# k and q projected together in three column chunks after the first FFN stage, with two G banks summed beside them

## The chip, the cores and the metric

The kernel runs on one core of a Trainium2 chip. A core has a matrix engine (TensorE, "PE" in the profile, with its weight loads as "PEld"), a vector engine (VectorE, "DVE"), a scalar engine for activation functions (ScalarE, "ACT"), a general engine (GpSimd, "POOL") and a queue engine (SyncE, "SP") that issues most transfers. TensorE writes its sums into eight PSUM banks of 128 partitions by 512 fp32 values. Sixteen DMA engines move data between DRAM and the on-chip SBUF. The metric is the device time of one execution in microseconds; lower is better.

## What is computed

For 2048 tokens x of width 640 (bf16) the output is a gated mix of a linear attention block with 32 heads of width 20 and a GEGLU feed-forward block with a hidden width of 1728:

```
qkv = x @ wqkv                                  # 640 -> 3*640
phi(t) = where(t > 0, t + 1, exp(t)) + 1e-6
kv  = sum over tokens of phi(k)^T v   (per head, 20x20);   z = sum over tokens of phi(k)
o   = (phi(q) @ kv) / (phi(q) . z + 1e-6)       (per head)
a   = o @ wo
b   = (gelu(x @ w_gate) * (x @ w_up)) @ w_down
g   = sigmoid(sum(x * gate_w));   out = g * a + (1 - g) * b
```

## The kernel before

**How it is tiled.** Tokens come in 16 tiles `t` of 128 and four quarters `q` of 512; the width 640 is five K-slices `dk` of 128; the hidden width is 14 f-tiles `ft`, the last of 64 columns. Two forms of x are needed: with tokens on partitions (`x_all`, `x_sb`) and transposed (`xT`). Quarters 1 to 3 of `xT` come from transposing DMA loads; quarter 0 is transposed on TensorE (`transpose_x`, L139) and copied out of PSUM by VectorE (K-slices 0 and 1) and ScalarE (2 to 4).

**v is never projected.** Since kv = phi(k)^T (x wv), the kernel sums G = x^T phi(k) over all tokens (`g_units`, L250), 640 by 640 in five row blocks and two column chunks of 512 and 128, one PSUM bank each, with 16 matmuls per bank. Then it multiplies by wv in head groups under a mask (`phase_KV`), and by wo (`phase_M`), which gives the matrix `M` that phi(q) is multiplied with in the end. z is summed on VectorE by 15 additions of [128 x 640] (`phase_Z`, L268) and replicated over partitions by a matmul with ones (`phase_Zrep`, L274). The denominators (`phase_D`) scale phi(q), which is then transposed by DMA into `pqT`.

**The feed-forward.** `phase_E(q, ft)` (L163) projects gate and up columns of an f-tile for one quarter: five matmuls of 512 columns into each of two banks, gelu on ScalarE, product on VectorE. `phase_FT` (quarters 0 to 2) and `phase_F` (quarter 3) sum the attention part and w_down into one bank and scale by 1 - g. The denominator's scale holds g/(1-g).

**k and q.** `phase_K(st)` (L206) projects one token tile's k in column chunks of 512 and 129; the 129th column of the second chunk is gate_w, so that x . gate_w comes out beside k, and exp of its negative goes to `eneg`. `phase_Q(st)` (L242) does q in 512 and 128. Each chunk passes through `phi` (L178): exp on ScalarE (L180), min and add on VectorE (L182), max and add from PSUM on VectorE (L185).

**The order of the work.** A planner orders each engine's instructions when the program is built, starting from the order in which they are written; inside `tc.manual_schedule` TensorE keeps the written order. It runs:

1. six warm-up matmuls on constants (`NWARM`, L117), which need no data;
2. `k_first` (L212), in written order: transposes of token tiles 0 and 1 with one filler matmul between them, k's first column chunk of both tiles K-slice by K-slice while wk arrives in three pieces (L95), the gate row turned into a column by a transpose (L231) and five POOL copies (L235), the second chunks, transposes of tiles 2 and 3;
3. k of tiles 2 and 3, q of tiles 0 to 3, then E of quarter 0 (14 f-tiles);
4. k of tiles 4 to 15, then q of tiles 4 to 15 with G's matmuls between them (a twelfth of G's columns after each tile) and the z additions, z's replication inside the last part of G;
5. KV, E of quarter 1 with M and the denominators, FT of quarter 0, and then E and FT or F by turns.

The transfers are issued in this order on SyncE's queue: x tile 0; wk in three pieces; x tiles 2 and 3; wq; gate and up weights in column pieces of 512, 512 and 640; their last 64 columns (`wgu`); three transposing loads; x of quarters 1 to 3; wv, wo, w_down. ScalarE's queue issues x tile 1 and the gate row.

## Time and profile before

| what | value |
|---|---|
| time, median of 3 runs | 279.5 us (279.43 to 279.55) |
| the profiled execution | 279.5 us, span 277.7 us from first to last instruction |
| TensorE busy | 272.2 us (98%) |
| VectorE busy | 143.3 us (52%) |
| ScalarE busy | 76.1 us (27%) |
| first transpose starts, first k matmul starts | 3.89 us, 5.14 us |
| E of quarter 0 | 17.84 to 46.97 us |
| KV starts | 101.63 us |
| transfers | 23.58 MB, mean 85 GB/s over the span |

How to read it: times of rows are microseconds from the start of the span. TensorE's matmuls are pipelined, so the length of one (379 ns for 512 columns) is longer than the interval between two; the interval is what a stage costs. VectorE's instructions also overlap by some tens of nanoseconds. The chain of waits follows the work that ended last back to the start; where its rows adjoin and name TensorE alone, TensorE sets the time.

### The profile page before, as it was taken

To read this page: it belongs to the slowest core of one execution; us is meant where nothing else is said; L and a number is where in the kernel's file an instruction comes from. 1 tells how busy PE (TensorE), PEld (TensorE's weight loads), DVE (VectorE), ACT (ScalarE), POOL (GpSimd) and SP (SyncE) were. 2 spreads that over 40 slices of the span, in tenths; PEclk is the share of its full clock that TensorE was granted. 3 is DMA by queue.
4 is the path that set the end of the run, shared out by engine and by line. 5 is a ranking of instruction groups with operands and counts; after the bars stand their busy time and mean duration, and the time that the engine had idled before them with its cause. 6 is when DMAs were issued, how large, how long until landed. Compare 5 with 4: busy or idle time off the path is not lost.

```text
span 277.7 us, 3993 instructions
## 1 busy us (share of the span) xinstructions
PE 272.2 (98%) x1522; PEld 139.0 (50%) x1548; DVE 143.3 (52%) x317; ACT 76.1 (27%) x167; POOL 5.2 (2%) x18
## 2 busy tenths in 40 slices
PE   8999999999999999999999999999999999999995
PEld 3554444555454584544444444444444444445774
DVE  0793223899944369999999542221112332101011
ACT  3662323764333352442100123210012222000100
POOL 5000000000000000000000000000000000000000
PEclk9999999999999999999999999999999999999999
DMA  7999999200100005343223540001112000021301
GB/s 217 360 355 205 235 341 287 96 2 0 1 4 0 0 2 142 69 113 75 51 50 69 104 133 3 0 0 29 30 38 94 2 0 0 19 40 38 118 26 47
DMA packets 43818, 23.58 MB, mean 85 GB/s; under 512 B 30808, under 2 KB 43672, under 8 KB 43800
## 3 DMA queue, kind: packets, MB, share of 16 engines
q1 hardware_dynamic: 43646, 23.17, 31.9%
q8 instruction: 12, 0.20, 0.3%
q10 hardware_dynamic: 154, 0.17, 0.2%
q14 instruction: 6, 0.05, 0.1%
HBM read 13.32 MB, written 2.63 MB: 57 GB/s over the span
## 4 chain that ended last, share of the span: by engine, by line
PE 96%; DMA 1%; ACT 1%; issue 1%; DVE 0%
PE ps_u L155 20%; PE ps_g L155 20%; PE ps_acc L378 16%; PE ps_q L192 8%; PE ps_G L255 8%; PE ps_k L192 7%; PE ps_acc L375 6%; PE ps_acc L398 5%; PE ps_acc L395 2%; PE ps_gu L155 2%; DMA x_all<-in_A_x_dram 1%; PE ps_k L218 1%; PE ps_m L332 1%; PE ps_kv L304 1%; ACT phi_e L180 0%
## 5 line engine op out<-in xcount | busy, mean ns | idle before, releaser
L160 ACT ACTIVATE gl<-ps_g 128x512 bf16<-128x512 f32 x52 | 31.1, 597 | 112.1 <-PE ps_g L155 111.3
L155 PEld LDWEIGHTS <-wu 128*128 128x128 bf16 x260 | 25.5, 98 | 30.7
L155 PEld LDWEIGHTS <-wg 128*128 128x128 bf16 x260 | 25.2, 98 | 29.1 <-issue 0.3
L161 DVE TENSOR_TENSOR hT_158<-ps_u,gl 128x512 bf16<-128x512 f32 x26 | 17.9, 690 | 31.9 <-PE ps_u L155 31.9
L378 PEld LDWEIGHTS <-wd 128*128 128x128 bf16 x210 | 20.5, 98 | 24.8
L378 PE MATMUL ps_acc<-hT_158,wd 128*128 128x512 bf16 x137 | 31.7, 379 | 0.2
L381 DVE TENSOR_TENSOR oT<-ps_acc,omg_rep 128x512 bf16<-128x512 f32 x15 | 10.3, 687 | 36.7 <-PE ps_acc L378 32.8
L161 DVE TENSOR_TENSOR hT_1371<-ps_u,gl 128x512 bf16<-128x512 f32 x26 | 17.8, 685 | 19.1 <-PE ps_u L155 19.1
L182 DVE TENSOR_SCALAR phi_m<-phi_e 128x512 bf16<-128x512 bf16 x64 | 12.9, 237 | 15.4 <-ACT phi_e L180 15.2
L180 ACT ACTIVATE phi_e<-ps_q 128x512 bf16<-128x512 f32 (+1 forms) x32 | 12.4, 435 | 21.6 <-PE ps_q L192 21.1
L398 PE MATMUL ps_acc<-wd,hT_1371 128*128 128x320 bf16 (+1 forms) x126 | 16.7, 284 | 0.0
L155 PE MATMUL ps_g<-xT_89,wg 128*128 128x512 bf16 x62 | 16.0, 379 | 0.2
L155 PE MATMUL ps_u<-xT_88,wu 128*128 128x512 bf16 x65 | 16.2, 379 | 0.0
L155 PE MATMUL ps_u<-xT_90,wu 128*128 128x512 bf16 x65 | 16.2, 379 | 0.0
L155 PE MATMUL ps_u<-xT_89,wu 128*128 128x512 bf16 x65 | 16.1, 379 | 0.0
L155 PE MATMUL ps_u<-xT_91,wu 128*128 128x512 bf16 x65 | 16.1, 379 | 0.0
L155 PE MATMUL ps_g<-xT_88,wg 128*128 128x512 bf16 x63 | 16.0, 379 | 0.1
L155 PE MATMUL ps_g<-xT_90,wg 128*128 128x512 bf16 x62 | 16.0, 379 | 0.2
L155 PE MATMUL ps_g<-xT_91,wg 128*128 128x512 bf16 x62 | 16.0, 379 | 0.2
L378 PE MATMUL ps_acc<-hT_1371,wd 128*128 128x512 bf16 x68 | 15.8, 379 | 0.1
L255 PEld LDWEIGHTS <-x_all 128*128 128x128 bf16 x160 | 12.0, 98 | 7.2
L180 ACT ACTIVATE phi_e<-ps_k 128x512 bf16<-128x512 f32 (+1 forms) x32 | 12.8, 439 | 7.5 <-PE ps_k L192 4.3
(142 smaller groups left out, 301.0 us busy)
## 6 DMA issues: line engine op xcount, KB each, us to landing
wd<-in_B_w_down_dram SPq DMA_DIRECT2D x1, 2080.0 KB
x_all<-in_A_x_dram SPq DMA_DIRECT2D x3, 640.0 KB, 4.8
out_dram<-o_q SPq DMA_DIRECT2D x3, 640.0 KB
wg<-in_B_w_gate_dram SPq DMA_DIRECT2D x2, 640.0 KB
wu<-in_B_w_up_dram SPq DMA_DIRECT2D x2, 640.0 KB, 10.2
wq<-in_A_wqkv_dram SPq DMA_DIRECT2D x1, 800.0 KB
wg<-in_B_w_gate_dram SPq DMA_DIRECT2D x1, 800.0 KB
wu<-in_B_w_up_dram SPq DMA_DIRECT2D x1, 800.0 KB
```

The source lines that it names most:

```text
L155: nc.tensor.matmul(ps[:, t0 : t0 + tw], lhsT=w[:, dk, ft * P : (ft + 1) * P], rhs=xT[q][:, dk, t0 : t0 + tw], start=(dk == 0), stop=(dk == ...
L160: nc.scalar.activation(out=gl[:], in_=psg[:], func=ACT.Gelu_apprx_tanh)
L161: nc.vector.tensor_tensor(out=hT_cur[q][:, ft, :], in0=psu[:], in1=gl[:], op=ALU.mult)
L180: nc.scalar.activation(out=e[:, :width], in_=src, func=ACT.Exp)
L182: nc.vector.tensor_scalar(out=m[:, :width], in0=e[:, :width], scalar1=1.0, scalar2=EPS, op0=ALU.min, op1=ALU.add,)
L192: nc.tensor.matmul(ps[:, 0 : hi - lo], lhsT=xT[q][:, dk, sl * P : (sl + 1) * P], rhs=w[:, dk, lo:hi], start=(dk == 0), stop=(dk == ND - 1),)
L255: nc.tensor.matmul(gp[:, 0 : hi - lo], lhsT=x_all[:, st, ct * P : (ct + 1) * P], rhs=pk[st][:, lo:hi], start=(st == 0), stop=(st == NT - 1),)
L375: nc.tensor.matmul(acc[:], lhsT=M["sb"][:, dk, ds], rhs=pqT[q][:, dk, :], start=(dk == 0), stop=False)
L378: nc.tensor.matmul(acc[:], lhsT=wd[:, ft, ds], rhs=hT[:, ft, :], start=False, stop=(ft == NF - 1))
L381: nc.vector.tensor_tensor(out=oT[:, 0:QW], in0=acc[:], in1=gsc["rep"][:, q * QW : (q + 1) * QW], op=ALU.mult)
L395: nc.tensor.matmul(acc[:, 0 : hi - lo], lhsT=pqT[q][:, dk, ts], rhs=M["sb"][:, dk, lo:hi], start=(dk == 0), stop=False)
L398: nc.tensor.matmul(acc[:, 0 : hi - lo], lhsT=hT[:, ft, ts], rhs=wd[:, ft, lo:hi], start=False, stop=(ft == NF - 1))
```

## The change

Quarter 0's E comes first and all of k and q after it, in one loop. wk, the gate column and wq become one tile `wqk` of 1281 columns, and `phase_KQ(st)` projects a token tile's k, gate and q in three column chunks of 512, 512 and 257, five matmuls each; phi's exp and min-add run per chunk, and the max-add is split where k ends and q begins. Beside this loop, two of G's ten banks are summed, one tile behind; the other eight follow when all k are done, and z is replicated after G. The transposes of quarter 0 go by pairs of token tiles into two banks with three copies (two on VectorE, one on ScalarE), and there is no written order for TensorE any more. The first two f-tiles of E run in halves of 256 tokens. There are seven warm-up matmuls.

On SyncE's queue stand now: x of tiles 0 and 1 in one transfer; 256 columns each of the gate and up weights; x of tiles 2 and 3; the further columns; `wgu`; wk; the gate column, element by element; the three transposing loads; wq; the rest as before. ScalarE's queue issues none. The ScalarE table that is loaded at the start is gelu's. `M`'s two tiles lie in one.

In the built program, the planner places one z addition beside each token tile of the new loop, from the second tile on, and z's replication between the last G matmul and KV. VectorE's second copy of a transposed pair waits for ScalarE's copy from the same bank.

```diff
-    NWARM = 6
+    NWARM = 7
...
-    wk = ov.tile([P, ND, D + P], BF16, name="wk", tag="slab_c")
-    wq = ov.tile([P, ND, D], BF16, name="wq", tag="slab_d")
+    WQK = 2 * D + 1
+    wqk = ov.tile([P, ND, WQK], BF16, name="wqk", tag="slab_c")
...
-    nc.scalar.dma_start(out=x_sb[0][:, 1, :], in_=x_view[:, 1, :])
-    nc.scalar.dma_start(out=gw5[:], in_=gate_w.rearrange("(k p) -> k p", p=P))
-    dma(out=x_sb[0][:, 0, :], in_=x_view[:, 0, :])
-    for lo, hi in ((0, 1), (1, 3), (3, 5)):
-        dma(out=wk[:, lo:hi, 0:D], in_=wqkv_v[:, lo:hi, D : 2 * D])
+    dma(out=x_sb[0][:, 0:2, :], in_=x_view[:, 0:2, :])
+    dma(out=wg[:, :, 0:256], in_=wg_v[:, :, 0:256])
+    dma(out=wu[:, :, 0:256], in_=wu_v[:, :, 0:256])
     dma(out=x_sb[0][:, 2:4, :], in_=x_view[:, 2:4, :])
-    dma(out=wq[:], in_=wqkv_v[:, :, 0:D])
...
-    for lo, hi in ((0, 512), (512, 1024), (1024, FM)):
+    for lo, hi in ((256, 512), (512, 1024), (1024, FM)):
...
+    dma(out=wqk[:, :, 0:D], in_=wqkv_v[:, :, D : 2 * D])
+    with nc.allow_non_contiguous_dma(reason="tiny gate_w column load"):
+        dma(out=wqk[:, :, D : D + 1], in_=gate_w.rearrange("(k p o) -> p k o", p=P, o=1))
     for q in (1, 2, 3):
         nc.sync.dma_start_transpose(out=xT[q][:, :, :], in_=x2[q * QW : (q + 1) * QW, :])
+    dma(out=wqk[:, :, D + 1 : WQK], in_=wqkv_v[:, :, 0:D])
...
+    def transpose_x(pair):
+        t0 = 2 * pair
+        tpa = psum.tile([P, 2 * QW], BF16, name="tp_a", tag="ps")
+        tpb = psum.tile([P, 2 * QW], BF16, name="tp_b", tag="ps")
+        c0 = t0 * P
+        for dk in range(ND):
+            tp, o = (tpa, dk * 2 * P) if dk < 2 else (tpb, (dk - 2) * 2 * P)
+            for i in range(2):
+                nc.tensor.transpose(
+                    tp[:, o + i * P : o + (i + 1) * P], x_sb[0][:, t0 + i, dk * P : (dk + 1) * P], ident[:]
+                )
...
+    def phase_KQ(st):
+        dst = (pk[st], pq[st])
+        for ci, (lo, hi) in enumerate(((0, QW), (QW, 2 * QW), (2 * QW, WQK))):
+            w = hi - lo
+            ps = ps_tile("ps_kq")
+            proj(ps, st, lo, hi)
+            e = work.tile([P, QW], BF16, name="phi_e")
+            nc.scalar.activation(out=e[:, 0:w], in_=ps[:, 0:w], func=ACT.Exp)
+            m = work.tile([P, QW], BF16, name="phi_m")
+            nc.vector.tensor_scalar(
+                out=m[:, 0:w], in0=e[:, 0:w], scalar1=1.0, scalar2=EPS, op0=ALU.min, op1=ALU.add,
             )
+            if ci == 1:
+                nc.scalar.activation(
+                    out=eneg[:, st : st + 1], in_=ps[:, D - QW : D - QW + 1], func=ACT.Exp, scale=-1.0
+                )
+            for i, base in ((0, 0), (1, D + 1)):
+                a, z = max(lo, base), min(hi, base + D)
+                if a < z:
+                    nc.vector.scalar_tensor_tensor(
+                        out=dst[i][:, a - base : z - base], in0=ps[:, a - lo : z - lo], scalar=0.0,
+                        in1=m[:, a - lo : z - lo], op0=ALU.max, op1=ALU.add,
+                    )
...
-    with tc.manual_schedule(engines={mybir.EngineType.PE}):
-        k_first()
-    for st in (2, 3):
-        phase_K(st)
-    for st in range(4):
-        phase_Q(st)
-    for ft in range(NF):
+    transpose_x(0)
+    e01 = [(ps_tile("ps_g"), ps_tile("ps_u")) for _ in range(2)]
+    for ft in range(2):
+        e_mm(e01[ft][0], wg, ft, 0, 0, 256)
+    e_mm(e01[0][1], wu, 0, 0, 0, 256)
+    transpose_x(1)
+    e_mm(e01[1][1], wu, 1, 0, 0, 256)
+    for ft in range(2):
+        e_mm(e01[ft][0], wg, ft, 0, 256, 256)
+        e_mm(e01[ft][1], wu, ft, 0, 256, 256)
+        e_out(0, ft, *e01[ft])
+    for ft in range(2, NF):
         phase_E(0, ft)
-    for st in range(4, NT):
-        phase_K(st)
+
+    early = [(ps_tile("ps_G"), ct) for ct in range(2)]
+    for st in range(NT):
+        phase_KQ(st)
+        if st > 0:
+            for gp, ct in early:
+                g_mm(gp, ct, st - 1, 0, QW)
+    for gp, ct in early:
+        g_mm(gp, ct, NT - 1, 0, QW)
+        g_out(gp, ct, 0, QW)
     phase_gate()
-    gu = g_units()
...
+    for st in range(NT):
+        phase_Z(st)
+    for i, (ct, lo, hi) in enumerate([(ct, 0, QW) for ct in range(2, ND)] + [(ct, QW, D) for ct in range(ND)]):
+        gp = ps_tile("ps_G")
+        for st in range(NT):
+            g_mm(gp, ct, st, lo, hi)
+        g_out(gp, ct, lo, hi)
     phase_Zrep()
-    for w in gu:
-        pass
     phase_KV(0, 4)
```

## The prediction

> **What bounds the kernel now.** I read the busy times first, then the chain of waits in order of time, then single matmuls of the first ten microseconds, then VectorE's timeline and the transfers. Busy times and the chain both say TensorE:
>
> ```profile
> PE 272.2 (98%) x1522; PEld 139.0 (50%) x1548; DVE 143.3 (52%) x317; ACT 76.1 (27%) x167; POOL 5.2 (2%) x18
> ```
>
> ```profile
> 0.81 3.03 DMA x_all<-in_A_x_dram
> 3.89 0.71 PE tp_x L145 x5
> ...
> 16.75 1.09 PE ps_q L192 x8
> 17.84 1.08 PE ps_g L155 x5
> ...
> 46.97 1.58 PE ps_k L192 x11
> ...
> 62.23 1.09 PE ps_k L192 x8
> 63.32 1.36 PE ps_q L192 x10
> ...
> 97.95 1.73 PE ps_G L255 x31
> ...
> 101.63 1.10 PE ps_kv L304 x20
> ...
> 270.28 1.90 PE ps_acc L398 x14
> ```
>
> The columns are start, length and work. Five 512-column matmuls take 1.08 us, so 215.8 ns each; 14 of 320 columns take 1.90, 135.7 each; 31 of 128 columns take 1.73, 55.8 each. Counting with these prices, the first E stage (135 x 215.8 = 29.13 us) runs from 17.84 to 46.97 and the stage of q and G from 63.32 to 101.63 without a hole. So no time is to be won by removing waits after 17.84: only the columns that TensorE streams, and the start, can move the end.
>
> The start I put into one number, TensorE's "zero": the moment from which an unbroken full-speed stream would have produced the same position. At 17.84 the k and q of four token tiles are done. One tile of k costs (63.32 - 46.97)/12 = 1.363 us, one of q 1.36; four of both cost 10.89. The zero of the kernel before is 17.84 - 10.89 = 6.95 us. It holds everything lost at the start: loads, transposes, and the slow clock, which shows in the starts of single matmuls:
>
> ```profile
> 6.42 0.93 PE L218 MATMUL ps_k<-wk,xT_88 128*128 128x512 bf16 x3
> ...
> 6.75 0.60 PE L218 MATMUL ps_k<-wk,xT_88 128*128 128x512 bf16 x2
> ...
> 6.97 0.38 PE L218 MATMUL ps_k<-wk,xT_88 128*128 128x512 bf16 x1
> ```
>
> These are tails of one group, cut at different moments: starts at 6.42, 6.75, 6.97, so the interval falls from about 0.43 (5.14 to 5.57) to 0.22 us. Full speed comes near 6.7, 5.9 us after the first warm-up matmul at 0.85.
>
> **Columns streamed (k and q together).** Removed per tile: 1.363 + 1.36 = 2.72 us in 20 matmuls. Added: ten of 512 (2.158) and five of 257 columns; 257 lies between 128 (55.8) and 320 (135.7), so 109.6 ns each, 0.548. The sum 2.706 saves 0.017 a tile, 16 tiles: **-0.25 us**. G keeps its 80 + 80 matmuls. Twenty matmuls of the first two f-tiles become forty of 256 columns (109.2 by the same line): **+0.05 us**.
>
> **The start.** Out go the K-slice order, the two transfers on ScalarE's queue (x tile 1, gate row), the gate's transpose, five POOL copies that a k matmul awaited, and a filler matmul between transposes; all that is inside 6.95. SyncE's queue now carries x of tiles 0-1 (320 KB), two 256-column pieces of wg and wu (320 KB each), x of tiles 2-3, then the rest. Transposes begin when x lands; x tile 0 landed at 3.84, and the seventh warm-up matmul ends at 0.85 + 7 x 0.427 = 3.84, so I take 3.87. Ten transposes at 0.107 (five took 0.50 before the next start) end at 4.94. VectorE copies 512 columns (288 ns for 256 and 160 for 5, so about 0.42) until 4.95, and the first gate-projection matmul starts at 5.05 once wg is in: k's first weights landed 2.9 us after issue at 1.27, with 0.49 MB up to them; 0.16 MB more makes about 4.9. Ten matmuls of 256, 0.213 each until 6.7, then 0.109, end at 7.0; five of wu end at 7.55. The next thing late is x of tiles 2-3:
>
> ```profile
> x_all<-in_A_x_dram SPq DMA_DIRECT2D x1, 320.0 KB, 5.2
> ...
> wk<-in_A_wqkv_dram SPq DMA_DIRECT2D x1, 160.0 KB, 2.9
> ...
> omg_d<-omg_all SPq DMA_DIRECT2D x1, 8.0 KB, 10.7
> ```
>
> Before, it was issued at 2.74 and landed 5.2 later, 7.94, as the end of 1.47 MB. Now it ends 1.31 MB: 0.16 MB less at 380 GB/s is 7.5. But wg and wu come in 512-byte pieces, which no row shows. 320 KB cost 0.9 us by bytes at 365 GB/s; if each piece cost what a 1024-byte piece does (SyncE pushed 640 of those per 1.79 us), 1.79. The two wgu transfers, 640 pieces of 128 bytes each, fit into the last microsecond before the transposing loads (windows of 21 to 22 us), at most 0.5 each; a line from there to 1.79 gives 1.05 at 512 bytes. That is 0.15 too much, twice: landing at 7.8, bounds 7.5 and 9.3. From there: ten transposes at 0.056 (0.56), ScalarE's copy (starts 0.25 later, 0.39), and only then VectorE's second copy of that bank, which waits for ScalarE (0.42); behind it stand the later projection matmuls. That is 1.65 us to 9.45, with 24 matmuls of 256 done (2.62): zero at 6.83, bounds 6.5 and 8.3. Against 6.95: **-0.12 us**, bounds -0.45 and +1.35. Nothing of E starves later: f-tile 4 is due near 15.5, its columns land by 14.
>
> The Trainium skill ("TensorE: Matmul & The Clock Gate", Part 1 and Part 4) speaks against this: full clock follows a busy window of about 3.4 us, and transposes don't count as busy, so the pause of 1.2 us in true matmuls could push the switch a window later, to about 10 us. By that rule the zero would be about 8.1 and the sum +0.95 us instead of -0.3. The trace of before shows a pause with a filler inside it, and no case without.
>
> **The load of wqk.** wk moves behind E's weights, the gate column becomes 640 two-byte pieces, wq stands behind three transposing loads. The windows' bytes reach the 6.72 MB ahead of those loads at 22.0 us, and they end at 32.0. Now 0.82 MB less is ahead (-2.2) and four 512-byte transfers (+0.6): 20.4. The gate lies between 0.5 (a 128-byte transfer of 640 pieces) and 3.3 (640/2048 of the 10.7 that omg_d's 2048 pieces took to land); I take 1.0, nearer the first, since that transfer also reads DRAM into SBUF. Then 10.0, wq 2.2, and 1.4 until it is seen: 35.0. The second column chunk of tile 0 needs it at 6.83 + 29.18 + 1.08 = 37.1. Cost **0**, slack 2.1; at 3.3 it is late by 0.2. Everything on PE's queue stands behind that wait. The other loads (x 4-15, wv, wo, wd) slip by about a microsecond; wv's first use is at 101. "DMA: Bandwidth & Descriptors" (Rules for kernel authors) says that a non-contiguous last dimension becomes one descriptor per element; it has no price for that.
>
> **VectorE in the joint stage.** Six banks are left, and per tile eight instructions follow each other:
>
> ```profile
> 50.78 0.39 DVE L182 TENSOR_SCALAR phi_m<-phi_e 128x512 bf16<-128x512 bf16 x2
> 51.08 0.82 DVE L271 TENSOR_TENSOR zacc<-zacc,pk_77 128x640 f32<-128x640 f32 x1
> 51.81 0.88 DVE L185 SCALAR_TENSOR_TENSOR pk_77<-ps_k,phi_m 128x512 bf16<-128x512 f32 x2
> 52.61 0.59 DVE L182 TENSOR_SCALAR phi_m<-phi_e 128x512 bf16<-128x512 bf16 x3
> ```
>
> Start to start, not by length: 512 + 128 of phi_m 0.30 (0.20 + 0.10), z's add 0.73, 512 + 128 of the max-add 0.80 (0.60 + 0.20). By the same slopes 257 of phi_m is 0.13, 383 and 257 of the max-add 0.47 and 0.33. Sum 0.20 + 0.20 + 0.13 + 0.60 + 0.20 + 0.47 + 0.33 + 0.73 = 2.87 us a tile (the planner puts z's add beside each tile). TensorE needs 2.706 + 2 x 0.216 = 3.14. VectorE just fits; a bank is back about 2.3 us after its last matmul and wanted again after 6.3 - 1.1. Cost **0**; with the lengths instead of the intervals (3.54), +0.40 x 16 = 6.4. ScalarE: 2 x 0.60 + 0.17 + 0.39 = 1.76 a tile; its table load (1.28) at the seam is covered by five free banks.
>
> **After G.** z's replication now stands right before KV, so VectorE's denominators start about 1.9 us later than before against TensorE. It is busy from 100.6 to 154.5, and its first copy of a final sum (152.3) comes 14 us after that sum is done. 1.9 later, the second E group of 155 still finds a bank. **0**.
>
> **Sum.** -0.25 + 0.05 - 0.12 = -0.32 us. The profiled execution took 279.5 with a span of 277.7, 1.8 around it, and equals the median of 279.5: 279.5 - 0.3 = **279.2 us**. That is inside 0.2% (0.56 us), about what a measurement can tell from no change.
>
> **Rivals.**
> 1. Slower: the clock. The point is whether transposes alone from 3.87 to 5.05 keep the clock's count going. For it: full speed needed 5.9 us, and the filler matmul is gone. Against it: TensorE stands idle less than before (before: 0.48 us ahead of the first transpose). If the count starts again at 5.05, the first 30 half-width matmuls and ten transposes run at half speed up to 10.9: zero 8.1 to 8.4, +1.0 to +1.3, **280.6**. 27%.
> 2. Slower: the gate's pieces. Every microsecond beyond 3.1 is one of stall at 37.1. Should they take as long as omg_d's whole 10.7, 286.8; half of that, 281.4. 12%.
> 3. Slower: VectorE at full lengths, 285.6. 6%; the intervals speak against it.
> 4. Faster: wg and wu at byte speed, zero 6.5: -0.45 - 0.2 = -0.65, **278.85**. For it: wgu's pieces were quick. 18%.
> 5. No change, the sum above: 37%.
>
> The range takes in 1, 4, 5 and the nearer half of 2: 278.8 to 281.4; the likeliest alone is 278.95 to 280.05. Faster 0.18, same 0.37, slower 0.45.
>
> **What would show it.** Right: the first projection matmul near 5.05, matmuls of 256 columns at 0.11 from 6.7, the second transposes at 7.8, E's end near 36.0, the joint stage 3.14 us a tile with no wait on VectorE, G's end straight into KV. Wrong: 0.21 intervals past 7.5 (rival 1), a hole before the second chunk of tile 0 with wqk as its releaser (2), TensorE waiting on phi's max-add (3), the second transposes past 8.5.

## The result and the profile after

The changed kernel takes 280.45 us (median of 6 runs, 280.17 to 280.76), the kernel before 279.52 in the same series (6 runs, 279.10 to 280.11). The ratio is 1.0031 with a 95% interval of 1.0018 to 1.0044: 0.9 us slower, where 0.3 us faster was forecast. The profiled execution took 280.49 us with a span of 278.8. A second series, of 12 runs, gave 1.0026 (1.0007 to 1.0044). Times and ratios in this document leave out one slow execution, of 486.2 us at a mean granted clock of 0.559, in the first run with x ahead of the up weights.

TensorE's busy time is nearly what it was (272.4 us against 272.2), so 0.9 of the 1.1 us by which the span grew is time in which it stands idle. Page of the changed kernel, busy time, share and instructions by engine:

```profile
PE 272.4 (98%) x1463; PEld 139.4 (50%) x1487; DVE 143.9 (52%) x300; ACT 72.2 (26%) x148; POOL 4.5 (2%) x13
```

The chain of waits of the changed kernel (start, length, work) answers the rows shown of before:

```profile
2.40 6.06 DMA x_all<-in_A_x_dram
8.50 0.40 PE tp_a L146 x4
...
35.80 1.09 PE ps_gu L166 x5
...
86.20 0.70 DVE pk_79 L216
86.95 3.61 PE ps_G L224 x16
...
102.64 1.10 PE ps_kv L272 x20
...
271.29 1.90 PE ps_acc L366 x14
```

Three readings. First, the chain no longer begins with x's first tile and TensorE, but with the load of token tiles 2 and 3, which lands at 8.46 us. Second, E ends at 35.80 + 1.09 = 36.89, so the zero is 36.89 - 29.18 = 7.71 us, where 6.95 stood before and 6.83 was forecast. (A row of the chain begins where the work before it ends, 0.17 us behind the start that the timeline gives for E; the zeros in this document are all read from chains, as the 6.95 was.) Third, between E and G stands VectorE, and it releases a matmul of G at 86.95. KV starts at 102.64, 1.01 later than before (101.63), and the same 1.01 is still there near the end (271.29 against 270.28): nothing is lost or won after KV.

TensorE's timeline at the start of the changed kernel (start, length, matmuls; in brackets the idle time ahead and what ended it):

```profile
5.14 1.65 PE L166 MATMUL ps_g<-xT_87,wg 128*128 128x256 bf16 x10
7.57 0.72 PE L166 MATMUL ps_u<-xT_87,wu 128*128 128x256 bf16 x5 [0.78 <-DMA wu<-in_B_w_up_dram]
8.50 0.40 PE L146 MATMUL tp_a<-ident,x_all 128*128 128x128 bf16 x4 [0.21 <-DMA x_all<-in_A_x_dram]
```

E starts at 5.14 (5.05 forecast) and its first ten matmuls are done by 6.8 (7.0 forecast). Then TensorE waits for the up weights' piece and again for x.

At the other end of the stage, TensorE's timeline around token tile 15:

```profile
86.17 0.59 PE L224 MATMUL ps_G<-pk_79,x_all 128*128 128x512 bf16 x2
86.95 0.59 PE L224 MATMUL ps_G<-pk_79,x_all 128*128 128x512 bf16 x2 [0.18 <-DVE pk_79 L216]
```

The second pair starts 0.78 after the first, in place of two times 0.216: a wait of 0.35 us for VectorE's max-add of tile 15. (The bracket counts idle time only from the modelled end of the matmul before.)

### The profile page after: what moved, and what is told of

Same layout as the page of the kernel before. It is cut to its first block, busy times and chain, and to the rows that moved or that the text cites. A ratio compares the mean times of both kernels' runs of the same rounds, so it can differ in the third digit from the quotient of the medians.

```text
span 278.8 us, 3785 instructions
## 1 busy us (share of the span) xinstructions
PE 272.4 (98%) x1463; PEld 139.4 (50%) x1487; DVE 143.9 (52%) x300; ACT 72.2 (26%) x148; POOL 4.5 (2%) x13
## 4 chain that ended last, share of the span: by engine, by line
PE 78%; DVE 16%; DMA 2%; ACT 1%; issue 1%; SPq 1%; DVEq 0%
PE ps_u L166 20%; PE ps_g L166 20%; PE ps_acc L346 16%; PE ps_acc L343 6%; PE ps_G L224 6%; PE ps_acc L366 5%; DVE zacc L239 4%; DVE phi_m L206 3%; DMA x_all<-in_A_x_dram 2%; PE ps_acc L363 2%; PE ps_gu L166 2%; DVE pk_78 L216 1%; DVE pk_79 L216 1%; DVE pk_76 L216 1%; DVE pk_77 L216 1%
## 5 line engine op out<-in xcount | busy, mean ns | idle before, releaser
L166 PEld LDWEIGHTS <-wu 128*128 128x128 bf16 x270 | 26.3, 98 | 30.7 <-DMA wu<-in_B_w_up_dram 1.1
L166 PEld LDWEIGHTS <-wg 128*128 128x128 bf16 x270 | 26.1, 98 | 28.7 <-issue 0.7
L204 ACT ACTIVATE phi_e<-ps_kq 128x512 bf16<-128x512 f32 (+1 forms) x48 | 24.5, 528 | 23.4 <-PE ps_kq L192 17.6
L166 PE MATMUL ps_u<-xT_87,wu 128*128 128x512 bf16 (+1 forms) x75 | 16.7, 351 | 0.8 <-DMA wu<-in_B_w_up_dram 0.8
L166 PE MATMUL ps_g<-xT_87,wg 128*128 128x512 bf16 (+1 forms) x72 | 16.7, 349 | 0.2
L166 PE MATMUL ps_g<-xT_88,wg 128*128 128x512 bf16 x62 | 16.0, 379 | 0.2
L166 PE MATMUL ps_u<-xT_88,wu 128*128 128x512 bf16 x65 | 16.2, 379 | 0.0
L166 PE MATMUL ps_u<-xT_89,wu 128*128 128x512 bf16 x65 | 16.2, 379 | 0.0
L166 PE MATMUL ps_u<-xT_90,wu 128*128 128x512 bf16 x65 | 16.1, 379 | 0.0
L166 PE MATMUL ps_g<-xT_89,wg 128*128 128x512 bf16 x62 | 16.0, 379 | 0.2
L166 PE MATMUL ps_g<-xT_90,wg 128*128 128x512 bf16 x62 | 16.0, 379 | 0.2
L366 PEld LDWEIGHTS <-hT_1210 128*128 128x128 bf16 x126 | 11.6, 98 | 3.7
L206 DVE TENSOR_SCALAR phi_m<-phi_e 128x512 bf16<-128x512 bf16 (+1 forms) x48 | 12.4, 265 | 1.7 <-ACT phi_e L204 1.6
```

The costliest lines, as they stand in the source:

```text
L166: nc.tensor.matmul(ps[:, t0 : t0 + tw], lhsT=w[:, dk, ft * P : (ft + 1) * P], rhs=xT[q][:, dk, t0 : t0 + tw], start=(dk == 0), stop=(dk == ...
L204: nc.scalar.activation(out=e[:, 0:w], in_=ps[:, 0:w], func=ACT.Exp)
L206: nc.vector.tensor_scalar(out=m[:, 0:w], in0=e[:, 0:w], scalar1=1.0, scalar2=EPS, op0=ALU.min, op1=ALU.add,)
L366: nc.tensor.matmul(acc[:, 0 : hi - lo], lhsT=hT[:, ft, ts], rhs=wd[:, ft, lo:hi], start=False, stop=(ft == NF - 1))
```

## The experiments

One table carries what the traces of all runs say about the two places. The landing is that of x of token tiles 2 and 3; the zero is E's end less the 29.18 us of E's matmuls (29.13 in the two kernels with x first, whose first f-tiles run in full width); "E to KV" is the time from E's end to KV's first matmul, so that start and loop are read apart.

| kernel | landing | zero | E to KV | ratio to before, 95% |
|---|---|---|---|---|
| changed | 8.46 | 7.71 | 65.75 | 1.0031 (1.0018 to 1.0044) |
| changed, second series | 7.95 | 7.21 | 65.74 | 1.0026 (1.0007 to 1.0044) |
| changed start alone | 8.85 | 8.09 | 65.54 | 1.0028 (1.0017 to 1.0039) |
| joint loop alone | - | - | - | 1.0120 (1.0097 to 1.0144) |
| z after the loop | 8.92 | 8.16 | 65.42 | 1.0015 (0.9999 to 1.0031) |
| z between | 8.11 | 7.36 | 65.45 | 1.0007 (0.9990 to 1.0024) |
| pieces of 2560 bytes | 7.93 | 7.19 | 65.74 | 0.9994 (0.9979 to 1.0008) |
| the same again | 8.04 | 7.29 | 65.75 | 1.0002 (0.9987 to 1.0017) |
| their control, 512 bytes | 8.19 | 7.45 | 65.75 | 1.0023 (1.0009 to 1.0038) |
| x first, z after | 4.9 | 8.76 | 65.42 | 0.9993 (0.9972 to 1.0014) |
| x first, filled | by 5.2 | 7.07 | 65.46 | 1.0004 (0.9987 to 1.0020) |
| x before up, z after | 6.84 | 7.26 | 65.42 | 0.9999 (0.9981 to 1.0017) |
| x before up, three banks | 7.48 | 7.50 | 65.46 | 0.9989 (0.9969 to 1.0009) |

The landing of one and the same start differs from execution to execution: 8.46, 7.95, 8.85, 8.92 and 8.11 in five profiles, mean 8.46. The zero follows it at a distance of 0.74 to 0.76 each time. So a single zero is good to about half a microsecond, while "E to KV" repeats to 0.04 us between kernels with the same loop. Where a start is judged, the timed series (11 or 12 runs in most) weigh more than one profile.

**The start alone.** The new start and load order, with the old stages behind it:

```diff
-    early = [(ps_tile("ps_G"), ct) for ct in range(2)]
-    for st in range(NT):
-        phase_KQ(st)
...
+    for st in range(NT):
+        phase_K(st)
+    for st in range(4):
+        phase_Q(st)
+    phase_gate()
+    gu = g_units()
```

> The changed start and order of loads (E of quarter 0 first, x by pairs, 256-column pieces of wg and wu first), with the stages of the kernel before behind it: all 16 k tiles, q of tiles 0 to 3, then q and G by turns, z as before; wk and wq are separate tiles. My theory: two terms went wrong, the start and the joint loop. The zero of the changed kernel is 7.71 us against 6.95 (E ends at 36.89, less 135 x 216 ns), so this kernel pays +0.76 and +0.05 for the half matmuls and nothing in the loop: KV starts near 102.4, time 280.3, ratio 1.003. The rival, that the loop is the cause: E still ends near 36.9, but the later stages run from buffers that are early anyway and KV is back near 101.6, time 279.5. If both terms are real and additive, this kernel and the one with the joint loop alone add up to the whole change (+0.93).

Measured: 280.68 us against 279.86 of the kernel before, ratio 1.0028. From its chain:

```profile
2.39 6.46 DMA x_all<-in_A_x_dram
...
36.19 1.08 PE ps_gu L166 x5
37.27 21.80 PE ps_k L203 x160
...
102.81 1.10 PE ps_kv L285 x20
```

No row of VectorE stands between E and KV, and the stages take 65.54 us, the sum of their columns (16 x 2.723 + 21.73 + 0.27 = 65.57). The time is 0.8 us over the kernel before with nothing of the joint loop in it. So the start carries nearly the whole loss, and the loop as a whole only 65.75 - 65.54 = +0.2.

**The joint loop alone.** The old start; the joint loop for tiles 4 to 15, with wk and wq in one tile `wqk`:

```diff
-    wk = ov.tile([P, ND, D + P], BF16, name="wk", tag="slab_c")
-    wq = ov.tile([P, ND, D], BF16, name="wq", tag="slab_d")
+    wqk = ov.tile([P, ND, WQK], BF16, name="wqk", tag="slab_c")
+    wk = wqk[:, :, 0 : D + 1]
+    wq = wqk[:, :, D + 1 : WQK]
...
+    for st in range(4, NT):
+        phase_KQ(st)
+        for s2 in range(4) if st == 4 else (st - 1,):
+            for gp, ct in early:
+                g_mm(gp, ct, s2, 0, QW)
```

> The start of the kernel before (k and q of tiles 0 to 3 by the old code, then E), and the joint loop for tiles 4 to 15 with two early G banks, the other eight after it, z additions beside the loop, z's replication after G. My theory: the columns give 12 x 0.017 = -0.2 us; VectorE is busy without a break through the loop (period 3.19 us a tile in the changed kernel's trace against TensorE's 3.14) and makes the last two early G matmuls wait, 0.35 us in the changed kernel; here the eight extra G matmuls after tile 4 (1.73 us) give VectorE time, so 0 to 0.2 of it: KV 101.4 to 101.65, time 279.3 to 279.55. The rival, that the loop carries the whole loss: KV near 102.4, time 280.3.

Measured: 282.8 us, ratio 1.0120; both theories missed. The edit did more than it meant to. TensorE's timeline, and then the rows of half a microsecond (busy time and count of PE, PEld, DVE, ACT, POOL, then the granted clock, DMA share, GB/s):

```profile
10.89 0.69 PE L220 MATMUL ps_k<-wqk,xT 128*128 128x129 bf16 x5 [2.42 <-POOL wqk L237]
```

```profile
12.00:12.50 0.50, 0.50 (x9) 0.36 (x7) 0.50 (x2) 0.50 (x2) 0.00 (x0) 0.87 1.11 352
12.50:13.00 0.50, 0.50 (x3) 0.10 (x2) 0.50 (x4) 0.50 (x3) 0.00 (x0) 0.50 1.12 354
...
15.00:15.50 0.50, 0.50 (x3) 0.15 (x1) 0.28 (x2) 0.41 (x3) 0.00 (x0) 0.50 1.13 358
15.50:16.00 0.50, 0.50 (x3) 0.20 (x2) 0.50 (x3) 0.00 (x0) 0.00 (x0) 0.71 1.07 338
```

In the common tile the gate column lies between k's and q's columns, and POOL's copy of it waited for the transfer of wq, which landed at 10.52. TensorE stood for 2.42 us. By the means of the first and the last of these rows (0.87 and 0.71), the granted clock then fell to 0.50 at 12.37, 1.5 us after TensorE had resumed, and stayed there until 15.79, for 3.4 us. E starts at 22.28 instead of 17.84. The profile shows a long execution: it and one more of the six took 284.2 us at a mean clock of 0.993, the other four 282.45 to 282.95 at 1.000, which is the 2.42 and the loop's 0.33 (below) and no more. So the wait cost a second time, through the clock, in two executions of six. That was not expected.

The later part of the same trace still answers the question: E ends at 51.42 and KV starts at 106.41, 54.99 us, against 46.97 to 101.63 before, 54.66. So the loop for twelve tiles costs +0.33 and saves nothing net, although its chunks stream fewer columns; VectorE releases G's last early matmul here too.

**The z additions after the loop.** One pin that keeps them behind all of k and q:

```diff
-        nc.vector.tensor_tensor(out=(zsum[:] if st == NT - 1 else zacc[:]), in0=(pk[0][:] if st == 1 else zacc[:]),
-                                in1=pk[st][:], op=ALU.add)
+        add = nc.vector.tensor_tensor(out=(zsum[:] if st == NT - 1 else zacc[:]), in0=(pk[0][:] if st == 1 else zacc[:]),
+                                      in1=pk[st][:], op=ALU.add)
+        if st == 1:
+            tc.keep_in_program_order(add)
```

> The changed kernel with the 15 additions of z held back until all of k and q is done, nothing else. My theory: VectorE's 3.19 us a tile (0.73 of it z's addition) is what makes G's matmul of tile 15 wait until 86.95; without the addition VectorE needs 2.46 a tile, G(15) starts at 86.60 without a wait, the 15 additions (11.0 us) end near 98.5, before z's replication at 102: KV at 102.3, time 280.1, 0.35 faster than the changed kernel. The rival, that the wait at the end is only the latency of exp, min and max behind tile 15's last k matmuls and so stands in any order: G(15) at 86.9, KV at 102.6, time 280.45.

Measured: 280.4 us against 279.86, ratio 1.0015. The 280.1 that was expected is missed, but in this series the kernel before took 0.34 more as well: 0.54 over it, where the changed kernel had 0.93, is 0.39 less, and 0.35 was expected (the two intervals overlap). The stage did what the theory says; its chain:

```profile
84.09 2.71 PE ps_kq L192 x15
86.80 15.69 PE ps_G L224 x132
...
102.76 1.10 PE ps_kv L274 x20
```

No wait ahead of G, 65.42 us in place of 65.75: VectorE's load in the loop cost 0.33 us.

**The same VectorE work in another order.** Is it the load, or the order in which the planner put it? The instructions of the loop, z's addition among them, are written so that none reads what the one right ahead of it wrote. The third chunk's max-add waits in `later` until the next tile's first min-add is out, and z's addition stands between the second chunk's min-add and max-add:

```diff
+            if ci == 0 and later:
+                later.pop()()
             if ci == 1:
...
+                if st > 1:
+                    phase_Z(st - 1)
+
+            def max_add(ci=ci, lo=lo, hi=hi, ps=ps, m=m):
...
+            if ci == 2:
+                later.append(max_add)
+            else:
+                max_add()
...
+    with tc.manual_schedule(engines={mybir.EngineType.DVE}):
         for st in range(NT):
             phase_KQ(st)
```

> The changed kernel with the same VectorE work in the joint loop, the z addition too, in another written order: no instruction stands right behind the one whose result it reads. Per tile: min-add 512, max-add 257 of the tile before, max-add 512, min-add 512, z's addition, max-add 128, max-add 383, min-add 257. In the changed kernel three pairs stand in direct succession, and its start-to-start times are 0.24 + 0.69 + 0.21 + 0.10 (nothing) + 0.29 + 0.47 + 0.14 + 0.73 + 0.33 = 3.19 us. My theory: the excess over my forecast of 2.87 lies in these pairs (max-add 512 at 0.69 in place of 0.60, max-add 128 at 0.29 in place of 0.20, the hole of 0.10): in the new order the period VectorE could keep is 2.9 to 3.0, it falls into step with TensorE's 3.14, G's matmul of tile 15 does not wait, and E's end to KV takes 65.3 to 65.4 us in place of 65.75. The rival, that these instructions are as long in any order because matmuls and exp use the same memory at the time: period 3.15 or more, wait 0.3 to 0.4, 65.7 us. The start is that of the changed kernel, so the time is 280.0 to 280.2 or 280.45.

Measured: 280.04 us against 279.78, ratio 1.0007. VectorE's timeline of the changed kernel, one tile and the next one's first row (start, length, instruction):

```profile
66.75 0.28 DVE L206 TENSOR_SCALAR phi_m<-phi_e 128x512 bf16<-128x512 bf16 x1
67.07 0.69 DVE L216 SCALAR_TENSOR_TENSOR pk_78<-ps_kq,phi_m 128x512 bf16<-128x512 f32 x1
67.68 0.28 DVE L206 TENSOR_SCALAR phi_m<-phi_e 128x512 bf16<-128x512 bf16 x1
68.06 0.29 DVE L216 SCALAR_TENSOR_TENSOR pk_78<-ps_kq,phi_m 128x128 bf16<-128x128 f32 x1
68.27 0.55 DVE L216 SCALAR_TENSOR_TENSOR pq_100<-ps_kq,phi_m 128x383 bf16<-128x383 f32 x1
68.74 0.22 DVE L206 TENSOR_SCALAR phi_m<-phi_e 128x257 bf16<-128x257 bf16 x1
68.87 0.82 DVE L239 TENSOR_TENSOR zacc<-zacc,pk_78 128x640 f32<-128x640 f32 x1
69.61 0.42 DVE L216 SCALAR_TENSOR_TENSOR pq_100<-ps_kq,phi_m 128x257 bf16<-128x257 f32 x1
69.94 0.28 DVE L206 TENSOR_SCALAR phi_m<-phi_e 128x512 bf16<-128x512 bf16 x1
```

and of the reordered kernel:

```profile
59.87 0.29 DVE L208 TENSOR_SCALAR phi_m<-phi_e 128x512 bf16<-128x512 bf16 x1 [0.18 <-ACT phi_e L206]
60.08 0.42 DVE L224 SCALAR_TENSOR_TENSOR pq<-ps_kq,phi_m 128x257 bf16<-128x257 f32 x1
60.41 0.68 DVE L224 SCALAR_TENSOR_TENSOR pk<-ps_kq,phi_m 128x512 bf16<-128x512 f32 x1
61.01 0.28 DVE L208 TENSOR_SCALAR phi_m<-phi_e 128x512 bf16<-128x512 bf16 x1
61.21 0.82 DVE L252 TENSOR_TENSOR zacc<-zacc,pk 128x640 f32<-128x640 f32 x1
61.94 0.28 DVE L224 SCALAR_TENSOR_TENSOR pk<-ps_kq,phi_m 128x128 bf16<-128x128 f32 x1
62.14 0.55 DVE L224 SCALAR_TENSOR_TENSOR pq<-ps_kq,phi_m 128x383 bf16<-128x383 f32 x1
62.61 0.22 DVE L208 TENSOR_SCALAR phi_m<-phi_e 128x257 bf16<-128x257 bf16 x1
63.01 0.29 DVE L208 TENSOR_SCALAR phi_m<-phi_e 128x512 bf16<-128x512 bf16 x1 [0.18 <-ACT phi_e L206]
```

The lengths are the same to a hundredth; the starts are not. In the changed kernel the period is 69.94 - 66.75 = 3.19 us. A min-add of 512 is followed after 0.32 and 0.38 by the max-add that reads it. These two steps are the only ones of the eight that differ by more than 0.02: in the reordered kernel the same min-add is followed after 0.21 and 0.20 by something else. There the starts run 0.21, 0.33, 0.60, 0.20, 0.73, 0.20, 0.47, 0.14: 2.88 us of work in a period of 3.14, and now VectorE waits 0.18 per tile for ScalarE. E to KV falls to 65.45. So the planner's order cost 0.30 us, and the forecast's 2.87 was the price of an order that was not the built one.

The Trainium skill ("VectorE: DVE Perf Modes", section "The DRAIN you can't avoid") says that the next operation does not start until the pipe is empty, but also that one that is not held starts earlier. The rows agree with the second sentence: an independent instruction starts 0.08 us before the min-add ends (60.08 against 60.16), the max-add that reads the result 0.04 and 0.10 us after it (67.07 against 67.03, 68.06 against 67.96). What reading the result costs, 0.11 and 0.18 us here, is measured, not taken from the page.

**Longer pieces.** The first two weight transfers read 2560 bytes a partition in one run, from wo, in place of five runs of 512 from wg and wu (the kernel then computes something else and serves for its time only):

```diff
-    dma(out=wg[:, :, 0:256], in_=wg_v[:, :, 0:256])
-    dma(out=wu[:, :, 0:256], in_=wu_v[:, :, 0:256])
+    dma(out=wgA[:].rearrange("p k n -> p (k n)"), in_=A_wo[0:256, :].rearrange("(p r) n -> p (r n)", r=2))
+    dma(out=wuA[:].rearrange("p k n -> p (k n)"), in_=A_wo[256:512, :].rearrange("(p r) n -> p (r n)", r=2))
```

> The changed kernel, but the first two 320 KB weight transfers read one run of 2560 bytes a partition out of wo in place of five runs of 512 bytes, into tiles of their own; f-tiles 0 and 1 of every quarter therefore use other weights than the reference. Bytes, order and TensorE work stay. Theory A, the pieces of 512 bytes are slow (bytes moved per us between 3 and 8 us after the start were 236 to 355 GB/s, against 236 to 383 before): wu lands near 6.6 in place of 7.53, x of tiles 2 and 3 near 7.5 in place of 8.46, E ends near 36.1, time 279.7. Theory B, the landing is late because of what else is under way (later transfers that share the engines), whatever the pieces: wu 7.3 to 7.5, x of tiles 2 and 3 8.2 to 8.5, E ends 36.7 to 36.9, time 280.3 to 280.5.

Measured: 279.84 us against 279.86, ratio 0.9994: 0.8 us faster than the start-alone kernel timed beside it. But its landing, 7.93, is no earlier than the earliest of the changed start. So it was run again, beside a control that reads the same tensor in runs of 512 bytes:

```diff
-    dma(out=wgA[:].rearrange("p k n -> p (k n)"), in_=A_wo[0:256, :].rearrange("(p r) n -> p (r n)", r=2))
-    dma(out=wuA[:].rearrange("p k n -> p (k n)"), in_=A_wo[256:512, :].rearrange("(p r) n -> p (r n)", r=2))
+    dma(out=wgA[:], in_=A_wo[:, 0:256].rearrange("(k p) n -> p k n", p=P))
+    dma(out=wuA[:], in_=A_wo[:, 256:512].rearrange("(k p) n -> p k n", p=P))
```

> A control for the run with long pieces: the same tiles and the same source tensor (wo in place of wg and wu for f-tiles 0 and 1 of every quarter, so the output is another), but read as five runs of 512 bytes a partition, as the changed kernel reads wg and wu. If the length of the pieces is the cause, this kernel is as slow as the changed one: time 0.7 to 1.1 us above the long-piece kernel beside it, x of tiles 2 and 3 landing at 8.1 to 8.9. If the other source made the long-piece kernel quick, both agree within 0.3 us.

> The kernel with runs of 2560 bytes once more, on the same chip as its control (f-tiles 0 and 1 use wo's values). Theory of the pieces: ratio to the kernel before 0.998 to 1.001 again, x of tiles 2 and 3 landing at 7.5 to 8.0. If the first measurement was the spread of landings (7.95 to 8.92 in five profiles of the changed start), the ratio comes out near 1.003.

Measured: 279.89 us with long pieces (1.0002, 0.9987 to 1.0017), 280.21 with 512 bytes (1.0023, 1.0009 to 1.0038), 279.77 before. The long pieces agree with their first series; the control lies with the changed kernel. The ratios differ by 0.0021 (0.6 us), the medians by 0.32, less than the 0.7 expected at least; the two intervals overlap. Over all series, the four that start with 512-byte pieces in the changed order (the changed kernel twice, its start alone, the control) stand at 1.0023 to 1.0031 and the two long ones at 0.9994 and 1.0002. So the length of the pieces costs something like 0.3 to 0.8 us, and most of the start's loss goes with it. What stays open is the rest of the landing: with long pieces it still was 7.93 and 8.04, not the 7.5 that bytes alone gave.

**x of all four tiles first.** The order x 0-1, x 2-3, wg, wu, both pairs transposed before E, E in full width, z after the loop:

```diff
+    dma(out=x_sb[0][:, 2:4, :], in_=x_view[:, 2:4, :])
     dma(out=wg[:, :, 0:256], in_=wg_v[:, :, 0:256])
     dma(out=wu[:, :, 0:256], in_=wu_v[:, :, 0:256])
-    dma(out=x_sb[0][:, 2:4, :], in_=x_view[:, 2:4, :])
```

> The changed kernel with z's additions after the loop, and x of tiles 2 and 3 loaded right behind tiles 0 and 1, then the 256-column pieces of wg and wu; both pairs are transposed before E, and the first two f-tiles run in full width. My theory: the n-th 320 KB transfer lands at 4.0, 5.1, 7.5 and 8.5 to 8.9 us whatever it holds, 0.3 to 0.4 earlier where a 512-byte one is replaced by x's 1280-byte pieces: wg near 7.0, ten gate matmuls of 216 ns until 9.2, wu there by then; zero 7.0 to 7.2, E ends 36.2 to 36.4, KV at 101.6 to 101.8, time 279.2 to 279.5. Against it: TensorE stands idle from 5.8 to 7.0, and in the kernel with the joint loop alone an idle time of 2.42 us was followed by 3.2 us of matmuls at half speed; if 1.2 us is enough for that, zero 8.5 and time 281.

Measured: 279.67 us against 279.78, ratio 0.9993. The profiled execution took 281.2 us, well over that median, so it shows a long execution, one of two: it and the longest (281.64) have a mean granted clock of 0.994, the other ten 0.998 or more. TensorE's timeline, and rows of its clock:

```profile
5.13 0.50 PE L146 MATMUL tp_b<-ident,x_all 128*128 128x128 bf16 x6
6.90 4.00 PE L166 MATMUL ps_g<-xT,wg 128*128 128x512 bf16 x10 [1.27 <-DMA wg<-in_B_w_gate_dram]
```

```profile
6.50:7.00 0.50, 0.10 (x1) 0.10 (x2) 0.00 (x0) 0.00 (x0) 0.00 (x0) 0.91 1.15 343
7.00:7.50 0.50, 0.50 (x2) 0.18 (x3) 0.00 (x0) 0.00 (x0) 0.00 (x0) 0.50 1.17 335
...
10.00:10.50 0.50, 0.50 (x3) 0.14 (x2) 0.00 (x0) 0.00 (x0) 0.00 (x0) 0.68 1.08 342
```

From 4.0 to 6.9 us there is no matmul but transposes, and then 1.27 us of nothing; by the means of 0.91 and 0.68 the clock is 0.50 from 6.91 to 10.32, 3.4 us, and the first ten E matmuls take 3.84 us in place of 2.16. So the outcome named as the risk is what two executions of twelve show, while the median lies where the theory had no fall of the clock. It resembles the forecast's first rival, in a kernel whose pause is longer than the changed kernel's.

**The same, with the pause filled.** Five matmuls on constants between the transposes and E, in written order on TensorE, and the reordered VectorE work in place of z after the loop:

```diff
+    with tc.manual_schedule(engines={mybir.EngineType.PE}):
+        transpose_x(0)
+        transpose_x(1)
+        for r in range(5):
+            nc.tensor.matmul(t[:], lhsT=nc.const_aps.tensor(1.0, [P, P], BF16),
+                             rhs=nc.const_aps.tensor(1.0, [P, QW], BF16), start=True, stop=True)
...
```

> x of all four token tiles of quarter 0 first, then the first weight pieces, as in the run before, with the VectorE order in which no instruction follows the one it reads from, and with five matmuls on constants (512 columns each) between the last transposes and E. In the run without them the granted clock fell to 0.50 at 6.95 us and stayed there until 10.3, after 2.9 us in which TensorE ran only transposes and then stood idle for 1.27 us. My theory: it is the lack of matmuls that lets the clock fall; the fillers (1.08 us at full speed, from 5.65 to 6.75) keep it, E's first ten matmuls take 2.16 us in place of 3.84, zero 6.9 to 7.0, E ends 36.1 to 36.2, KV 101.5, time 279.1 to 279.3. The rival, that the clock falls for another reason (time since the start, or the power of the matmuls themselves): rows of 0.50 again, E ends 37 or later, time above 280.5.

Measured: 279.82 us against 279.71, ratio 1.0004, and the twelve times lie within 279.52 to 280.32. TensorE's timeline:

```profile
5.81 1.25 PE L395 MATMUL warm_ps<-const-bfloat16-1.0 128*128 128x512 bf16 x5
6.91 2.32 PE L166 MATMUL ps_g<-xT,wg 128*128 128x512 bf16 x10
```

Ten matmuls from 6.91 to 9.06 at full speed; zero 7.07, KV at 101.66. The clock stays up, and no execution of the twelve is long. That the fillers did it is not shown by this: without them the clock stayed up in ten of twelve as well, and the two profiles differ in when it first came up (six transposes take 0.84 us from 4.57 here, 0.50 us from 4.25 there). KV stands where it stood in the kernel before (101.63), and the time agrees with that kernel's on this chip. The 279.1 to 279.3 that was expected is missed: the zero came out 0.1 higher, and the stage took 65.46, not 65.3.

**x ahead of the up weights.** Two runs with the order x 0-1, wg, x 2-3, wu, the second one with the reordered VectorE work and a third PSUM bank for a transposed pair:

```diff
     dma(out=wg[:, :, 0:256], in_=wg_v[:, :, 0:256])
+    dma(out=x_sb[0][:, 2:4, :], in_=x_view[:, 2:4, :])
     dma(out=wu[:, :, 0:256], in_=wu_v[:, :, 0:256])
-    dma(out=x_sb[0][:, 2:4, :], in_=x_view[:, 2:4, :])
...
+        tpc = psum.tile([P, 2 * QW], BF16, name="tp_c", tag="ps")
```

> The changed kernel with z's additions after the loop, and x of tiles 2 and 3 loaded ahead of the up weights' first piece; TensorE does the gate halves of tokens 0-255, the second transposes, the gate halves of tokens 256-511, then up in full width. My theory: x of tiles 2 and 3 lands near 7.1 to 7.4 (third in place of fourth), transposes until 7.9 to 8.1, ten gate halves of 109 ns until 9.0 to 9.3 with wu there by then: zero 6.9 to 7.2, E ends 36.1 to 36.4, KV 101.5 to 101.8, time 279.1 to 279.5. The rival, that the fourth transfer's landing (8.5 to 8.9) still decides because up is then late: E ends 36.6 or later, time 279.8 or more.

> x of tiles 2 and 3 ahead of the up weights' first piece, as in the earlier run, with the VectorE order in which no instruction follows the one it reads from, and with a third PSUM bank for the transposed pairs, so that VectorE's second copy does not wait for ScalarE's copy out of the same bank. In the earlier run TensorE waited 0.18 and 0.19 us for VectorE's two copies, and some 0.4 us stood open between 7.6 and 8.55. My theory: the second copy goes 0.4 earlier, zero 6.85 to 6.95 in place of 7.26, E ends 36.0 to 36.15, KV 101.35 to 101.55, time 279.0 to 279.3 (before 279.5 to 279.8 by chip). If the landings alone decide, the zero stays at 7.2 and the time at 279.6.

Measured: 279.73 us against 279.78 (0.9999) and 279.76 against 279.71 (0.9989, 0.9969 to 1.0009). In the first, x landed at 6.84, and TensorE waited for the copies, not for the load; zero 7.26. In the second, the wait for VectorE's second copy (0.19 us) is gone and that for its first (0.18) is still there, but x landed at 7.48 in the profiled execution, TensorE waited 1.09 us for it, and the zero is 7.50. The bank's gain is therefore not shown. Both take back the whole loss of the changed kernel; neither is shown to be faster than the kernel before.

**The changed kernel again.**

> The changed kernel once more, unchanged, beside these two on one chip: the same start has shown landings of x of tiles 2 and 3 at 8.46, 8.85, 8.92 and 8.11 us in four kernels. If the landing is what moves the time, its profile shows a zero 0.75 above the landing's distance as before (landing less 0.75), E's end to KV at 65.75 whatever the landing, and a time of 280.3 to 280.7, 1.0 us above the two others.

Measured: 280.52 us, ratio 1.0026, landing 7.95, zero 7.21, E to KV 65.74: the expectation held, except that the two kernels beside it were 0.7 and 0.8 ahead by the medians, not 1.0.

## Why the prediction was wrong

The forecast had six terms, three of them zero; KV's start measures their sum in the traces. Measured: 102.64 - 101.63 = +1.01 us in the profiled execution, +0.93 by the medians, where -0.32 was forecast.

| term | forecast | measured |
|---|---|---|
| start ("zero" 6.83 against 6.95) | -0.12 | +0.76 (7.71; mean of five profiles 7.71, 7.21 to 8.16) |
| halves of the first two f-tiles | +0.05 | taken as forecast (in the 29.18 of E), not told apart |
| columns of k and q | -0.25 | about -0.1 (E to KV without a wait against the old stages) |
| VectorE in the joint stage | 0 | +0.30 to +0.33 (reordered, and z after the loop) |
| gate column and wqk's load | 0 | 0: no wait ahead of the second chunk |
| after G | 0 | 0: +1.01 at KV and +1.01 in the last sums |

**The start: the landing was mis-sized.** The step "0.16 MB less at 380 GB/s is 7.5 ... landing at 7.8" failed; the mean is 8.46. It had two premises. One was that a transfer lands when the bytes up to it have moved. The rows of bytes speak against it. Windows of one microsecond, the last number in GB/s, of the changed kernel and of the kernel before:

```profile
6.00:7.00 1.00, 0.71 (x6) 0.38 (x4) 0.03 (x1) 0.00 (x0) 0.00 (x0) 1.00 1.04 325
7.00:8.00 1.00, 0.43 (x4) 0.40 (x5) 0.00 (x0) 0.00 (x0) 0.00 (x0) 1.00 1.13 323
```

```profile
6.00:7.00 1.00, 1.00 (x5) 0.37 (x3) 0.00 (x0) 0.00 (x0) 0.00 (x0) 1.00 1.05 380
7.00:8.00 1.00, 1.00 (x6) 0.40 (x5) 0.16 (x1) 0.00 (x0) 0.28 (x3) 1.00 1.07 383
```

Summed from 2 us on, the changed kernel had moved 192 + 355 + 236 + 274 + 325 + 323 = 1705 KB by 8.0 and some 1.85 MB by 8.46, although x of tiles 2 and 3 ends the first 1.31 MB. The kernel before had also moved about 1.86 MB when it landed at 7.94, with 1.47 MB up to it. So 0.4 to 0.5 MB issued behind it had moved beside it, and fewer bytes ahead did not bring it forward. The total is no rule either: in the other four executions of this start the rows sum to 1.73 MB (landing 7.95), 1.79 (8.11), 1.95 (8.85) and 1.95 MB (8.92). The traces' single packets show where the spread lies. Those of x are the only ones of 1280 bytes before 10 us; in the five executions half of the 256 packets of tiles 2 and 3 had started by 5.99 to 6.28 us, but the last one ended at 7.48 to 8.38, and the landing came 0.46 to 0.54 later. So the last few packets decide, and they differ from execution to execution; why they are late stays open. No run tried to hold the later transfers back, so this part is read from the traces and not shown by an experiment.

The other premise was the price of 512-byte pieces, 0.15 us for each transfer. By the timed series the two transfers cost 0.3 to 0.8 us together. The rows alone would not show it: the rate is 323 to 325 GB/s against 380 to 383 before, but the kernel with long pieces has 337 and 329 in the same two windows (the next pieces of wg and wu have 512 bytes in both). The bound of 9.3, from the 1024-byte pieces' row, did cover the landing.

**The start: two ways of reading.** The term missed by 0.88 us (-0.12 forecast, +0.76 measured), and the landing (8.46 for 7.8) is 0.66 of it. Another 0.17 lay in the subtraction: 6.83 was counted from the starts of matmuls, but the 6.95 that it was compared with came from the chain, where E begins at 17.84. The timeline of the kernel before:

```profile
17.67 1.24 PE L155 MATMUL ps_g<-xT_88,wg 128*128 128x512 bf16 x5
```

From starts the old zero is 17.67 - 10.89 = 6.78, so the forecast's own numbers gave +0.05, not -0.12. Behind the landing the forecast was right. VectorE's second copy waited for ScalarE's, as it said:

```profile
9.68 0.42 DVE L155 COPY xT_87<-tp_b 128x512 bf16<-128x512 bf16 x1 [0.31 <-ACT xT_87 L152]
```

It ended at 10.10, 1.64 us behind the landing (1.65 forecast), and the 25th matmul of 256 columns started at 10.15, with the forecast's 24 done.

**VectorE: the intervals belonged to another order.** "VectorE just fits" came from start-to-start intervals in a stage where no instruction follows the one it reads; summed to 2.87, they were right to 0.02 for such an order (2.88 measured). But the term was put at zero without the order that the planner built, and that order has such pairs. The max-adds of k's first chunk show three stretches. From 45.41 to 54.39 they start 2.99 us apart, and VectorE makes up for its late start (its first min-add is at 39.45, behind gelu's last tile, the table load of 1.28 and the first exp). From 54.39 to 60.68 they follow in TensorE's own step of 3.14. From 63.88 to 86.20, tiles 8 to 15, each tile has the two pairs shown above and needs 3.19; seven steps of 0.05 too much are the 0.35 us that the last early G matmul pays. Rival 3 named the mechanism, but priced it by the full lengths as 6 us.

**The columns: mis-sized.** E to KV without any wait is 65.42 to 65.46, against 65.54 for the old stages behind the same start: 0.1 saved, not 0.25 (16 x 0.017 is 0.27). With z after the loop, the 16 joint tiles and 14 pairs of G matmuls between them run from 37.34 to 86.80: (49.46 - 28 x 0.2157) / 16 = 2.714 us a tile, where 2.706 was summed. A saving of 0.017 is the difference of two sums of 2.7, and 0.008 of error in one of them takes half of it.

**What held, and what did not matter.** E's first matmuls were to stand 0.213 us apart until 6.7. They stand 0.11 apart from the first one on, so the clock was up by 5.14 in this execution, and what held them up was a copy:

```profile
5.14 0.49 PE L166 MATMUL ps_g<-xT_87,wg 128*128 128x256 bf16 x3
```

```profile
5.61 0.42 DVE L155 COPY xT_87<-tp_b 128x512 bf16<-128x512 bf16 x1 [0.52 <-ACT xT_87 L152]
```

One of these matmuls is 0.27 long, so three in 0.49 us start 0.11 apart; the last five of the ten start at 6.08 only, behind the copy's end at 6.03. That the ten ended near the forecast's 7.0 all the same was luck, and it cost nothing, since the up weights landed at 7.53. (The profile's clock column reads 1.00 from 0 us on, even where the warm-up matmuls start 0.427 apart, so ahead of E only starts show the clock.) No row at half clock comes later in this profile, and the mean clock is 0.998 or more in all 18 timed executions of the changed kernel: rival 1 did not happen here. Two other kernels of this study show that the clock can fall behind a pause. The Trainium skill ("TensorE: Matmul & The Clock Gate", Part 1) gives a window of about 3.4 us; the two stretches at 0.50 lasted 3.4 us each, which agrees. A pause of 2.42 us brought one about in two executions of six. Rival 2 did not happen: no wait for wqk.

**The range.** 278.8 to 281.4 held 280.45; "slower" had the largest of the three chances, but mostly for the clock and the gate column, not for the landing and VectorE's order.

## What to carry to other kernels

At the start of a kernel, transfers issued later move beside the one that is waited for, and the last packets of a transfer can come long after most of it. So do not estimate a landing from the bytes ahead; take it from the same kind of transfer in several executions, with its spread. Before two moments are subtracted, see that both are read in the same way, from starts or from the chain. An engine that "just fits" must be costed in the order that is built: look for instructions that read what the one right ahead wrote, and put independent work between. And when TensorE will pause for two to three microseconds, for whatever reason, reckon with a half-speed stretch of 3.4 us behind the pause in some executions. Matmuls on constants in the pause went with none in twelve executions here, which does not yet show that they prevent it.

## What the runs showed that was not expected

- On VectorE the start-to-start time after a 512-column min-add is 0.20 to 0.21 us when the next instruction is independent, and 0.32 to 0.38 when it reads the result; two such pairs cost 0.3 us a tile (3.19 against 2.88).
- A pause of 2.42 us on TensorE, and another of 2.9 us with nothing but transposes in it, were followed by 3.4 us at a granted clock of 0.50 in two executions of six and two of twelve, in the first case only 1.5 us after work had resumed.
- The landing of the same fourth transfer varied from 7.95 to 8.92 us between executions, which is as wide as the whole effect under study; the stage behind it repeated to 0.04 us. Half of its packets had started by 5.99 to 6.28 us each time.
- One tile for two weight matrices tied a copy of one column to the transfer of the other matrix, and cost 2.42 us of waiting at once.
